# Three decay rows copied by GpSimd instead of VectorE, and one pair's query transposes moved two tiles earlier

## The chip, the cores and the metric

The kernel runs on one core of a Trainium2 chip. The core has five engines that take their instructions in order and wait for one another through semaphores: TensorE (PE, with its weight loads shown apart as PEld), VectorE (DVE), ScalarE (ACT), GpSimd (POOL) and SyncE (SP). The metric is the device time of one execution in microseconds (us). Most of it is the span that the profile shows; a little lies around the span.

## The reference

Eight batches of eight heads of causal attention with a forgetting gate (576 positions, head size 64), and behind it an MLP of 512 to 2048 to 512 on the 4608 tokens:

```python
scores = scale * np.matmul(q, k.transpose(0, 1, 3, 2))
cum = np.cumsum(np.log(np.clip(f, 0.0001, 1.0)), axis=-1)
scores = scores + cum[:, :, :, None] - cum[:, :, None, :]      # causal part only
attn = exp(scores - max) / (sum + 1e-09)
x = (attn @ v) as (B * S, H * D)
h = x @ w_in
out = (h - np.tanh(h)) @ w_out
```

## The kernel before

**The decay.** The scores are one matrix product over 67 rows: 64 rows of the head and three more that bring in the decay. K carries a high part of `cum`, a low part and ones; Q carries two rows of minus ones and the high part. `KT[0]` and `QT[0]` hold the 67 rows for each head of batch 0. At the start ACT takes the logarithm of `f` (L184), VectorE sums it up (the scan, L187) and makes the two parts `chi` (L189) and `clo` (L190), 67 partitions by 576. Head 0 is served first: partitions 64 to 66 of `clo` are its three K rows, and VectorE copies them into `KT[0]` (L191, a 3x576 copy). The rows of heads 1 to 7 are laid out by three DMAs in `bulk()`: the high and the low rows of K from SP (L211, L213), the high row of Q from GpSimd's queue (L212).

**Pairs and tiles.** The heads are worked through in pairs, 32 in all; pair p is heads 2c and 2c+1 of batch b. The loop over `p` (L658) emits a slot for each pair: seven score tiles, `scores(b, c, ti)`, and between them whatever else is due. Tiles 0 to 2 belong to the pair's first head, tile 3 is the tail of both heads (the last 64 keys, written to `EL`), tiles 4 to 6 belong to the second head. Each tile is one or two products on PE (L352), a mask product in batch 0 (L355) and an exponential on ACT (L361) that reads the PSUM bank and writes the tile `e`. Two PSUM banks are shared by the score tiles of batch 0, and a third, `tr`, by every third tile, by the tail of slot 0 and by products that nobody reads (`unread`, L566).

**Turning queries and keys.** Batch 0 comes in rows, and `trans()` turns a pair's queries or keys: six transposes on PE (L298) into a PSUM bank, then two copies of 64x576 (L309 on ACT, L311 on VectorE), for the even and the odd positions. The string `copies` says which engine takes which half ("AV": ACT first, VectorE second). Strings listed in line 314 emit only the first half at once and put the second into the list `LATER`, which `rest()` empties. In slot 0 the keys of pair 1 are turned behind tile 2, the queries of pair 2 behind tile 5; from slot 1 on, the queries of pair p+2 behind tile 5 and the keys of pair p+1 behind tile 0.

**What feeds it.** GpSimd issues the loads of q, k, v and the weights (`load_qk`, L102; `load_v_block`, L131; `load_win`, L222) from one queue, in the order in which they are emitted: heads 0 to 3 of q and k, three loads of v, a mask (L169), the high row of Q (L212), then heads 4 and 5 of q (needed by the turn of pair 2's queries), heads 4 and 5 of k, heads 6 and 7, and the blocks of v.

`start()` turns pair 0, emits its first two score tiles and fills PE with `unread` while the decay is made; `bulk()` follows, then the slots. From slot 4 on the MLP's products fill PE.

Of the kernel before, what the change touches and what calls it, by code (L numbers as in the profile page):

```python
# [21 lines left out]
def kernel(  # L22
# [10 lines left out]
    nc = tc.nc  # L33
    P = 128

    B, H, S, D = q.shape
    NH = B * H
# [3 lines left out]
    NPAIR = H // 2  # L41
# [28 lines left out]
    def m_bank(name):  # L70
        while M_AT[0] % 3 in KEPT:
            M_AT[0] += 1
        M_AT[0] += 1
        return ps_m.tile([P, 512], FP32, tag=f"m{(M_AT[0] - 1) % 3}", name=name)
# [18 lines left out]
    qn, kn = ([t[0:S // NT6, :].rearrange("p (h n d) -> p h n d", h=H, n=NT6) for t in raw] for raw in (qraw, kraw))  # L93
    qb, kb = ([t[:, 0:NJ * DM].rearrange("p (n e) -> p n e", n=NJ) for t in raw] for raw in (qraw, kraw))
    vn = [qkp.tile([P, NJ, H, VW], FP16, tag=f"vn{i}", name=f"vn{i}") for i in range(2)]
    QT = [qkp.tile([D + 3, H, S], FP16, tag=f"QT{i}", name=f"QT{i}") for i in range(2)]
    KT = [qkp.tile([D + 3, H, PITCH], FP16, tag=f"KT{i}", name=f"KT{i}") for i in range(2)]
# [3 lines left out]
    def load_qk(dst, src, b, h0, h1):  # L101
        nc.gpsimd.dma_start(  # L102
            out=dst[b % 2][:, h0:h1, :, :].rearrange("p h n d -> p h (n d)"),
            in_=src[b, h0:h1, :, :].rearrange("h (p n) d -> p h (n d)", n=NT6))
# [25 lines left out]
    def load_v_block(b, n, h0, h1):  # L130
        nc.gpsimd.dma_start(out=vn[b % 2][:, n, h0:h1, 0:D],  # L131
                            in_=v[b, h0:h1, n * P:(n + 1) * P, :].rearrange("h p d -> p h d"))
# [3 lines left out]
    NX = NH + 3  # L136
# [23 lines left out]
    chi = cst.tile([NX, S], FP16)  # L160
    clo = cst.tile([NX, S], FP16)
# [26 lines left out]
                                 op0=ALU.mult, op1=ALU.add)  # L188
    nc.vector.tensor_scalar(out=chi, in0=cum, scalar1=mul_k, scalar2=add_k, op0=ALU.mult, op1=ALU.add)  # L189
    nc.vector.scalar_tensor_tensor(out=clo, in0=cum, scalar=mul_l, in1=chi, op0=ALU.mult, op1=ALU.subtract)  # L190
    nc.vector.tensor_copy(out=KT[0][NH:NX, 0, 0:S], in_=clo[NH:NX, :])  # L191

    def aug_rows(b):
        i, h0 = b % 2, 0 if b else 1
        hs = slice(b * H + h0, (b + 1) * H)
        return [(KT[i][D:D + 1, h0:H, 0:S], chi[hs, :]), (KT[i][D + 1:D + 2, h0:H, 0:S], clo[hs, :]), (QT[i][D + 2:D + 3, h0:H, :], chi[hs, :])]

    def load_aug(b):
        for to, of in aug_rows(b):
            nc.sync.dma_start(out=to, in_=of)  # L200

    def const_rows(i):
        h0 = 1 - i
        nc.sync.dma_start(out=QT[i][D:D + 2, h0:H, :], in_=minus16[0:2 * (H - h0), :])
        nc.sync.dma_start(out=KT[i][D + 2:D + 3, h0:H, 0:S], in_=ones16[0:H - h0, :])
# [1 line left out]
    const_rows(0)  # L207

    def bulk():
        (k_hi, chi_0), (k_lo, clo_0), (q_hi, _) = aug_rows(0)  # L210
        nc.sync.dma_start(out=k_hi, in_=chi_0)  # L211
        nc.gpsimd.dma_start(out=q_hi, in_=chi_0)  # L212
        nc.sync.dma_start(out=k_lo, in_=clo_0)  # L213
        load_qk(qn, q, 0, 4, 6)
        load_qk(kn, k, 0, 4, 6)
        load_qk(qn, q, 0, 6, H)
        load_qk(kn, k, 0, 6, H)
        for n in range(NJ - 1):
            load_v_block(0, n, 2, H)
# [67 lines left out]
    def trans(b, c, src, dst, early, copies, split=False):  # L287
        pn, g3 = S // NT6, NT6 // 2
        if early:
            t32 = m_bank("t32")  # L290
        elif KEPT and src is kn:
            t32 = ps_m.tile([P, UW], FP32, tag=f"m{KEPT[0]}", name="t32")
        else:
            t32 = ps_tr.tile([P, UW], FP32, tag="tr", name="t32")
        t16 = t32.bitcast(FP16)[:, 0:2 * S // 2].rearrange("p (a g n) -> p a g n", a=2, g=g3)
        for a in range(2):
            for g in range(g3):
                nc.tensor.transpose(out=t16[:, a, g, :],  # L298
                                    in_=src[b % 2][:, 2 * c + a, 2 * g:2 * g + 2, :],
                                    identity=id16[0:pn, 0:pn])  # L300
        parts = [(a, e) for a in range(2) for e in range(2)] if split else [(slice(0, 2), e) for e in range(2)]

        def copy(a, e, eng):
            if split:
                a = slice(a, a + 1)
            to = dst[b % 2][0:D, 2 * c:2 * c + 2, e:S:2].rearrange("d a (p g) -> d a p g", g=g3)[:, a]
            of = t16[e * D:(e + 1) * D, :, :, :].rearrange("d a g p -> d a p g")[:, a]
            if eng == "A":
                nc.scalar.activation(out=to, in_=of, func=AF.Copy)  # L309
            else:  # L310
                nc.vector.tensor_copy(out=to, in_=of)  # L311

        todo = [lambda a=a, e=e, eng=eng: copy(a, e, eng) for (a, e), eng in zip(parts, copies)]
        now = 1 if copies in ("VA", "Vv") else 2
        for fn in todo[:now]:
            fn()
        if now == 1:
            LATER.extend(todo[now:])
        return todo[now:]
# [54 lines left out]
    AV = {}  # L374
# [193 lines left out]
    pairs = [(b, c) for b in range(B) for c in range(NPAIR)]  # L568
# [22 lines left out]
    def att_items(p):  # L591
        def put(fn, *args):
            items.append((lambda: fn(*args), True))

        items = []
        here = pairs[p] if p < len(pairs) else None
        before = pairs[p - 1] if 0 < p <= len(pairs) else None
        after = pairs[p + 1] if p + 1 < len(pairs) else None
        early = p < NPAIR
        for ti in range(len(TILES)):  # L600
            if here and (p > 0 or ti > 1):
                put(scores, *here, ti)
            if p == 1 and ti == 6:
                items.append((lambda: const_rows(1), False))
                items.append((lambda: load_aug(1), False))
            if p == 0 and ti in (2, 5, 6):
                put(unread, {2: 6, 5: 4, 6: 2}[ti])
            if p == 1 and ti == 3:
                put(last)
            for load in LOADS.get((p, ti), ()):  # L610
                items.append((load, False))
            at_q, at_k = (1, 2) if p == 0 else (None, 0) if early else (0, 2) if p == NPAIR else (0, 3)
            if ti == 5 and p < NPAIR - 1:
                put(trans, *pairs[p + 2], qn, QT, True, "VV")
            if p in (2 * NPAIR - 1, 2 * NPAIR, 2 * NPAIR + 1) and (ti % 2 or ti == 0):
                items.append((rest, False))
            if p in (2 * NPAIR - 1, 2 * NPAIR) and ti % 2 == 0:
                pair = pairs[2 * NPAIR + 2 * (p - 2 * NPAIR + 1) + ti // 4]
                put(trans, *pair, *((kn, KT) if ti % 4 else (qn, QT)), False, "VA")
            if ti == at_q and p < 2 * NPAIR - 1:  # L620
                put(trans, *after, qn, QT, early, "VV")
            if p == NPAIR:
                if ti in (4, 5):
                    put(mlp1, 0, ti - 4, 1)
                    items.append((rest, False))
            if ti == at_k and p < 2 * NPAIR - 1 and p != NPAIR:
                put(trans, *after, kn, KT, early, "AV" if p in (0, 2) else "VV")
            if p == NPAIR:
                if ti == 0:
                    put(turn, *pairs[1])  # L630
                elif ti == 1:
                    put(turn, *pairs[p - 2])
                    put(values, *before)
                    put(mlp1, 0, 0, 0)
                elif ti == 2:
                    put(mlp1, 0, 1, 0)
                    put(turn, *before, True)
                    put(trans, *after, kn, KT, early, "Vv")
            elif early and ti in (2, 4) and before:
                put(values, *before, (ti // 2 - 1,))  # L640
            elif not early and ti == 2 and before:
                put(values, *before, (0, 1), p == NPAIR + 2)
            if p < NPAIR:
                if ti == 1 and p == 2:
                    put(turn, *pairs[0], True)
            elif p > NPAIR and ti == 3:
                items.append((release, False))
                put(turn, *before)
        return items
# [5 lines left out]
    at = 0  # L655
    start()
    bulk()
    for p in range(len(pairs) + 1):  # L658
        b, c = divmod(p, NPAIR)
        items = att_items(p)  # L660
# [53 lines left out]
```

## Time and profile before

| what | us |
| --- | --- |
| median of 3 runs (338.79 to 338.88) | 338.80 |
| the profiled execution, its own time | 338.77 |
| its span in the profile | 337.1 |
| around the span (338.77 - 337.1) | 1.67 |
| PE idle before the first score product, for VectorE's copy into K | 0.92 |
| POOL busy between 5 and 16 us | 10.86 of 11 |

The granted clock of TensorE is 1.00 in every stretch. The table's last two rows come from the view of waits and from the busy times by stretch. A line of the chain or the timeline begins with the start and the duration in us; square brackets give the idle time of the engine before the instruction and what ended it. A mean duration in a group is in ns.

### The profile page before, as it was taken

The numbers are of one execution on the slowest core, as the hardware profiler recorded it, in microseconds if no ns is written. First come the engines' busy times: TensorE is split into PE (matmuls) and PEld (weight loads), VectorE is DVE, ScalarE is ACT, GpSimd is POOL, SyncE is SP. The second block draws the span as 40 slices with busy tenths as digits, with TensorE's granted clock in tenths as the row PEclk, the third lists the DMA queues.
The fourth block names the chain that finished last, engine by engine and source line by source line (L and its number), as shares of the span: only waits on it lengthen the run. The fifth ranks groups of instructions, "written<-read, shape, count | busy, mean of one in ns | idle before, by whom it ended". The sixth has DMA issues, their size and how long they took to land.

```text
span 337.1 us, 8726 instructions
## 1 busy us (share of the span) xinstructions
PE 330.0 (98%) x3313; PEld 235.6 (70%) x3313; DVE 260.8 (77%) x509; ACT 233.2 (69%) x438; POOL 163.2 (48%) x321
## 2 busy tenths in 40 slices
PE   8899999999999999999999999999999999999996
PEld 8775558875687558845888888656865686486485
DVE  7998986659887886778867896788668866966865
ACT  6997777978977886788677867787558733632630
POOL 8977467775667564767377637722322210000000
PEclk9999999999999999999999999999999999999999
DMA  9999999999979997999899999990130022002003
GB/s 113 143 203 202 186 198 165 184 159 172 142 87 190 136 134 72 164 152 139 94 122 187 118 112 117 163 132 18 51 113 2 19 65 97 2 31 95 0 12 116
DMA packets 147468, 38.82 MB, mean 115 GB/s; under 512 B 128181, under 2 KB 146335, under 8 KB 147426
## 3 DMA queue, kind: packets, MB, share of 16 engines
q0 software_dynamic: 94528, 18.37, 75.5%
q1 hardware_dynamic: 52892, 19.89, 32.4%
q8 instruction: 26, 0.43, 0.6%
q14 instruction: 16, 0.13, 0.2%
q10 hardware_dynamic: 6, 0.01, 0.0%
HBM read 36.85 MB, written 9.44 MB: 137 GB/s over the span
## 4 chain that ended last, share of the span: by engine, by line
PE 90%; DVE 7%; ACT 2%; issue 1%; ACTq 0%
PE hps L451 36%; PE ops L517 29%; PE ps L352 11%; PE av L389 8%; PE ops L492 4%; DVE KT L311 2%; DVE QT L311 1%; PE t L298 1%; ACT e L361 1%; DVE xn L400 1%; DVE gq L462 0%; DVE TQ L187 0%; ACT th L456 0%; PE x L417 0%; DVE clo L190 0%
## 5 line engine op out<-in xcount | busy, mean ns | idle before, releaser
L451 PE MATMUL hps<-XR,win 128*128 128x512 f16 (+1 forms) x640 | 140.7, 357 | 0.3 <-DVE gq L462 0.3
L456 ACT ACTIVATE th<-hps 128x512 f32<-128x512 f32 x144 | 86.6, 602 | 55.5 <-PE hps L451 53.5
L361 ACT ACTIVATE e<-ps 128x512 f16<-128x512 f32 x192 | 110.2, 597 | 8.9 <-PE ps L352 7.4
L462 DVE TENSOR_TENSOR gq<-hps,th 128x512 f16<-128x512 f32 x144 | 98.0, 687 | 23.6 <-ACT th L456 22.0
L371 POOL TENSOR_SCALAR_AFFINE_SELECT e<-e 128x128 f16<-128x128 f16 x168 | 60.7, 364 | 71.5 <-ACT e L361 68.7
L451 PEld LDWEIGHTS <-win 128*128 128x128 f16 x640 | 57.7, 97 | 49.0 <-issue 1.1
L352 PE MATMUL ps<-QT,KT 67*128 67x64 f16 (+4 forms) x384 | 76.5, 276 | 2.0 <-DVE KT L311 1.4
L517 PEld LDWEIGHTS <-gq 128*128 128x128 f16 x640 | 60.3, 97 | 11.1
L517 PE MATMUL ops<-wout,gq 128*128 128x256 f16 x512 | 63.2, 272 | 0.0
L352 PEld LDWEIGHTS <-KT 67*128 67x128 f16 x384 | 36.4, 98 | 23.4 <-DVE KT L311 2.0
L389 PEld LDWEIGHTS <-e 128*128 128x128 f16 x896 | 32.3, 97 | 3.6
L389 PE MATMUL av<-vn,e 128*128 128x65 f16 x896 | 33.6, 193 | 0.0
L517 PE MATMUL ops<-W,sq 128*128 128x256 f16 x256 | 31.2, 272 | 0.0
L131 POOL DMA_DIRECT2D vn<-in_v_dram x32 | 28.0, 877 | 6.5 <-DMA win<-in_moe_w_in_dram 2.9
L400 DVE TENSOR_TENSOR xn<-av,rs 128x640 f16<-128x640 f32 x32 | 26.4, 825 | 1.3 <-DVE rs L399 0.2
L517 PEld LDWEIGHTS <-sq 128*128 128x128 f16 x256 | 24.1, 97 | 3.4
L108 POOL DMA_DIRECT2D kn<-in_k_dram x25 | 21.2, 848 | 2.1 <-issue 1.8
L108 POOL DMA_DIRECT2D qn<-in_q_dram x25 | 21.2, 848 | 1.8 <-issue 1.4
L371 POOL TENSOR_SCALAR_AFFINE_SELECT el<-el 128x128 f16<-128x128 f16 x28 | 9.3, 333 | 26.1 <-ACT el L361 25.8
L398 DVE TENSOR_SCALAR rs<-av 128x10 f32<-128x10 f32 x32 | 5.2, 163 | 18.2 <-PE av L389 17.0
L532 ACT ACTIVATE m<-ops 128x512 f32<-128x512 f32 x16 | 9.5, 596 | 10.9 <-PE ops L517 10.9
L484 DVE TENSOR_TENSOR gq<-gq 128x512 f16<-128x512 f16 x32 | 17.1, 533 | 0.0
(83 smaller groups left out, 311.8 us busy)
## 6 DMA issues: line engine op xcount, KB each, us to landing
out_dram<-ost SPq DMA_DIRECT2D x34, 256.0 KB
vn<-in_v_dram POOLq DMA_DIRECT2D x24, 128.0 KB, 6.2
qn<-in_q_dram POOLq DMA_DIRECT2D x20, 128.0 KB, 5.0
kn<-in_k_dram POOLq DMA_DIRECT2D x20, 128.0 KB, 5.6
win<-in_moe_w_in_dram POOLq DMA_DIRECT2D x2, 1024.0 KB, 11.8
wout<-in_moe_w_out_dram POOLq DMA_DIRECT2D x2, 1024.0 KB, 15.6
XR<-xn SPq DMA_TRANSPOSE x56
qn<-in_q_dram POOLq DMA_DIRECT2D x6, 144.0 KB, 4.6
```

Of the source, the lines that this page charges most:

```text
L108: nc.gpsimd.dma_start(out=dst[b % 2][0:pn, n, :].rearrange("p (h d) -> p h d", h=H), in_=src[b, :, n * P:n * P + pn, :].rearrange("h p d - ...
L131: nc.gpsimd.dma_start(out=vn[b % 2][:, n, h0:h1, 0:D], in_=v[b, h0:h1, n * P:(n + 1) * P, :].rearrange("h p d -> p h d"))
L352: nc.tensor.matmul(out=ps[:, col:col + n], lhsT=kt[0:rows, h, j * P:(j + 1) * P], rhs=qt[0:rows, h, i0:i0 + n], start=True, stop=cut == 0)
L361: nc.scalar.activation(out=e[:, lo:hi], in_=ps[:, lo:hi], func=AF.Exp, bias=-SHIFT, scale=qscale)
L371: nc.gpsimd.affine_select(out=view, in_=view, compare_op=ALU.is_ge, fill=0.0, base=0, pattern=pat, channel_multiplier=-1)
L389: nc.tensor.matmul(out=av[:, a, ib, :], lhsT=E.pop((b, c, a, j, ib)), rhs=vn[b % 2][:, j, 2 * c + a, 0:D + 1], start=(j == 0), stop=(j == ib))
L400: nc.vector.tensor_tensor(out=xn.rearrange("p i (a d) -> p a i d", a=2), in0=av[:, :, :, 0:D], in1=rs.to_broadcast([P, 2, NJ, D]), op=ALU. ...
L451: nc.tensor.matmul(out=hps[:, o:o + n], lhsT=win[:, ci, ft * P:(ft + 1) * P], rhs=XR[:, ci, t:t + n], start=(ci == 0), stop=(ci == NCH - 1))
L456: nc.scalar.activation(out=th, in_=hps, func=AF.Tanh, scale=-1.0)
L462: nc.vector.tensor_tensor(out=GQ[(u, i)][:, half, kt, :], in0=hps, in1=th, op=ALU.add)
L484: nc.vector.tensor_tensor(out=LHS[name](u, i)[:, ks], in0=LHS[x](u, i)[:, ks], in1=LHS[y](u, i)[:, ks], op=op)
L517: nc.tensor.matmul(out=ps[:, m, :], lhsT=LHS[lhs](u, kt // 4)[:, kt % 4, m * P:(m + 1) * P], rhs=rhs[:, kt, :], start=(fresh and (apart or ...
```

## The change

Three edits in the prologue and slot 0. First, the copy of head 0's three K rows goes from VectorE to GpSimd, and the DMA of Q's high rows, which `bulk()` issued, is now issued by GpSimd just ahead of that copy; the loads of heads 4 to 7 follow both. Second, the turn of pair 2's queries goes from behind tile 5 to behind tile 3 of slot 0, still on two VectorE copies. Third, of pair 1's keys only ACT's half is emitted at once; VectorE's half ("v" in "Av") is put into `LATER`, and so is the second half of pair 2's queries ("Vv"). `rest()` follows, so that VectorE's order in slot 0 becomes: queries of pair 2, first half; keys of pair 1, second half; queries of pair 2, second half.

```diff
-    nc.vector.tensor_copy(out=KT[0][NH:NX, 0, 0:S], in_=clo[NH:NX, :])
+    nc.gpsimd.dma_start(out=QT[0][D + 2:D + 3, 1:H, :], in_=chi[1:H, :])
+    nc.gpsimd.tensor_copy(out=KT[0][NH:NX, 0, 0:S], in_=clo[NH:NX, :])
...
     def bulk():
-        (k_hi, chi_0), (k_lo, clo_0), (q_hi, _) = aug_rows(0)
+        (k_hi, chi_0), (k_lo, clo_0), _ = aug_rows(0)
         nc.sync.dma_start(out=k_hi, in_=chi_0)
-        nc.gpsimd.dma_start(out=q_hi, in_=chi_0)
         nc.sync.dma_start(out=k_lo, in_=clo_0)
...
-        now = 1 if copies in ("VA", "Vv") else 2
+        now = 1 if copies in ("VA", "Vv", "Av") else 2
...
-            if ti == 5 and p < NPAIR - 1:
+            if ti == 5 and 0 < p < NPAIR - 1:
                 put(trans, *pairs[p + 2], qn, QT, True, "VV")
...
-                put(trans, *after, kn, KT, early, "AV" if p in (0, 2) else "VV")
+                put(trans, *after, kn, KT, early, "Av" if p == 0 else "AV" if p == 2 else "VV")
+            if p == 0 and ti == 3:
+                put(trans, *pairs[2], qn, QT, True, "Vv")
+                items.append((rest, False))
```

## The prediction

> **What bounds it now.** I read the page first, then the chain of work that ended last (0 to 60 us), then the timeline of 5 to 31 us, then the landing of single loads.
>
> ```profile
> span 337.1 us, 8726 instructions
> PE 330.0 (98%) x3313; PEld 235.6 (70%) x3313; DVE 260.8 (77%) x509; ACT 233.2 (69%) x438; POOL 163.2 (48%) x321
> ```
>
> PE's 98% hides the stage that matters here. The chain is on VectorE, with two steps on ACT and short ones on PE, from 0.9 to 26.09 us, and on PE for most of the time after it:
>
> ```profile
> 7.76 0.30 DVE KT L191
> 8.09 0.47 DVE KT L311
> 8.58 0.49 DVE KT L311
> 9.12 0.39 PE ps L352
> ...
> 11.38 0.81 ACT KT L309
> 12.22 0.81 DVE KT L311
> 13.05 0.79 DVE QT L311
> 13.86 0.81 DVE QT L311
> ...
> 26.09 0.45 PE x L417 x5
> ```
>
> All three edits lie between 7.7 and 14.7 us, so what counts is by how much the work at 26.09 us moves; the rest is taken to move with it. The reader should see L191 on the chain, and that VectorE's half of the keys waits for ACT's half. The timeline shows who else is full:
>
> ```profile
> 7.70 0.68 POOL L102 DMA_DIRECT2D qn<-in_q_dram  x1
> ...
> 12.20 3.39 ACT L361 ACTIVATE e<-ps 128x512 f16<-128x512 f32 x6
> 12.22 0.81 DVE L311 COPY KT<-t 64x576 f16<-64x576 f16 x1 [0.34 <-ACT KT L309]
> ...
> 16.50 1.68 ACT L361 ACTIVATE e<-ps 128x512 f16<-128x512 f32 x3 [0.19 <-PE ps L352]
> ...
> 28.41 0.60 ACT L361 ACTIVATE e<-ps 128x512 f16<-128x512 f32 x1 [0.98 <-PE ps L352]
> ```
>
> ACT runs from 9.60 to about 27 us with one gap of 0.19 us. It is nearly as tight as VectorE, so a late score tile costs as much as a late copy.
>
> **Edit 1, the copy to GpSimd.** VectorE loses 8.09 - 7.76 = 0.33 us. Its second K copy then ends at 8.74 instead of 9.07, and the first score product starts at 8.79 instead of 9.12. ACT is busy with pair 0's queries until 7.30 + 2.01 = 9.31, so the exponentials start at 9.31 instead of 9.60: the gain is 0.29 us.
>
> No copy on GpSimd is in the trace. The nearest rows are its memsets and selects:
>
> ```profile
> L586 POOL MEMSET KT<- 67x512 f16 x1 | 0.6, 599 | 0.0
> L169 POOL TENSOR_SCALAR_AFFINE_SELECT late<-late 128x128 f16<-128x128 f16 x1 | 0.5, 546 | 0.0
> L587 POOL MEMSET vn<- 64x528 f16 x1 | 0.5, 533 | 0.1
> L147 POOL TENSOR_SCALAR_AFFINE_SELECT id<-id 128x128 f16<-128x128 f16 x1 | 0.3, 294 | 0.7 <-DVE id L146 0.7
> ```
>
> The memsets took 599 ns for 512 elements and 533 ns for 528. I take 0.60 us for 576, nearest in length. The lower bound is VectorE's own 0.30 us for this copy. The upper bound takes the select's mean of 336 ns for 128 elements as all slope: 4.5 x 0.336 = 1.51 us. `clo` ends at 6.91 + 0.82 = 7.73; GpSimd answered VectorE 0.08 us late at the start (1.14 to 1.22), so the copy runs from 7.80 to 8.40. That is before 8.74, so VectorE's K copies hide it as far as score tile 0 goes.
>
> [...]
>
> **What stands behind it.** GpSimd's queue: the high rows of Q keep their place (issued at 7.17, as now), but the load of heads 4 and 5 of q goes from 7.70 to about 8.42, 0.72 us later, and so do heads 4 and 5 of k, heads 6 and 7, the v blocks and the first half of `win`. Those others have cover: k heads 4 and 5 landed at 8.37 + 3.6 = 11.97 and are turned at 13.78; the last v block at 12.70 + 4.9 = 17.6, first used at 18.32 (0.72 us, and the use moves too); `win` at 16.05 + 10.1 = 26.15, used at 27.28. The load of q heads 4 and 5 loses its cover, because edit 2 wants it sooner:
>
> ```profile
> L102 POOL DMA_DIRECT2D qn<-in_q_dram x1: 675/675/675, 7.7 to 7.7; - x1
> DMA to landing us min/median/max: 3.4/3.4/3.4
> ```
>
> It landed at 7.70 + 3.4 = 11.10 and was used at 12.57. The first load of the program, with nothing ahead of it, took 3.5 us, so 3.4 looks like a floor, not a queue. I forecast 8.42 + 3.4 = 11.82, and PE starts 0.07 later (first load: 1.55 + 3.5 = 5.05, weight load at 5.12): 11.89. Bounds for the landing: 11.10, if transfers ahead of it set it; 8.42 + 4.7 = 13.1, if it takes what loads with others in flight took.
>
> **Edit 2, the transposes behind tile 3.** PE gets there at 11.42 at the latest. The second half of tile 3 waited from 11.21 to 11.33 with no engine to wait for; I read that as head 1's low rows, issued by SP at 7.76, which don't move, so the 0.29 us gained may be lost here already. In either case PE stands still until 11.89, and queued behind it are tiles 4, 5 and 6 of pair 0, on which ACT waits. Six transposes take 0.27 us (12.57 to 12.84), so tile 4 starts at 12.16 and its exponential 0.48 us later (9.12 to 9.60): 12.64 instead of 12.20.
>
> **Edit 3, the order of the copies.** VectorE fills its idle 0.34 us only if the transposes are there. From 11.89 the first copy can start at 11.89 + 0.46 = 12.35 (9.80 to 10.26 is the pattern). With 0.81 each: queries 12.35 to 13.16, keys to 13.97, queries to 14.78 (14.67 before). Pair 1's first tile needs those keys: 14.02 instead of 13.50. Its exponential follows at 14.50 instead of 13.98.
>
> **Sum.** ACT is 0.52 us late at 13.98, and has no more idle time than 0.19 us, itself spent waiting for PE, which is late with it. VectorE's own stream is only 0.1 us late at 14.7, but its division for pair 0 (16.35) waits for PE's value products, which stand behind the late score tiles in PE's queue. So about 0.5 us reaches 26.09. Against the profiled execution: 338.77 + 0.52 = 339.29; its time is 0.03 below the median of the runs, so I say 339.3. With the copy at 0.30 us the landing is 11.52, PE starts at 11.59 and the same steps give +0.22; with 1.51 us the first tile starts 0.24 late and the transposes at 12.80: +1.43.
>
> **Rivals.** (a) *The load is there in time*: its landing is set by transfers ahead of it (the v load issued last before it landed at 10.7, Q's high rows at 10.87) and stays at 11.10. For it: the DMA engines show 9 tenths busy from 7 to 8.7 us. Against it: they fall to 4 to 6 tenths from 8.75 to 9.1, so the queue had run dry. Then VectorE's order works: first copy at 11.42 + 0.46 = 11.88, keys done at 13.50, tile 0 of pair 1 no later than now; with tile 3 moving up by 0.29 us, a gain of about 0.25. That is 338.5; at best both VectorE gains are earned, 0.33 + 0.34 = 0.67, 338.1. This one isn't slower.
>
> (b) *The copy is held up*: GpSimd's select of `late` took 546 ns while VectorE's `chi` ran to 6.88, and 294 ns for the same shape at 1.22; it ended 0.15 us behind `chi`. If VectorE's K copies hold GpSimd's copy likewise to 8.74, it ends at 9.35: first tile 0.28 late, the load issued 1.67 late, transposes near 12.85, +1.5: 340.3. It decides from a copy end of 8.74 on. Against it: between 7.76 and 8.38 GpSimd issued a load in 675 ns beside VectorE's copies.
>
> [...]
>
> (c) *The delay is absorbed*: only VectorE's 0.1 us counts and ACT's lateness ends in its idle 0.98 us at 27.4. For it: the chain names VectorE up to 26.05. Against it: PE's order ties the division to the score tiles. 338.9.
>
> **How the numbers follow.** Forecast 0.52 (338.9 to 339.8), (a) 0.17, (b) and longer waits 0.19, (c) 0.12. A measurement of this kernel tells about 0.2% from no change, 0.68 us: below 338.12 is faster, above 339.48 slower. Slower: all of (b) and nearly half of the forecast's share, since the landing can only be later than its floor, 0.19 + 0.24 = 0.43. Faster: under half of (a), 0.07. Within: 0.50. The range runs from the middle of (a) to (b): 338.3 to 340.4.
>
> **What would show it.** GpSimd's copy at 7.8, about 0.6 us long; the load of q heads 4 and 5 issued near 8.4 and landing near 11.8; PE idle before the transposes of pair 2's queries from 11.4 to 11.9; ACT idle ahead of tile 4, its exponential near 12.6; pair 1's first tile near 14.0; the first score product at 8.8. It is wrong if the load lands by 11.4, if the transposes wait for something other than the load, or if the starts at 26 us don't move as those at 14 do.

## The result, and the profile after

The changed kernel takes 339.64 us as a median of 22 executions (339.35 to 343.80); the kernel before takes 338.82 (338.79 to 339.10, also 22). The ratio is 1.0040 with a 95% interval of 1.0026 to 1.0054: slower. The medians are 0.82 us apart. The ratio of the means is larger, because four of the 22 executions took 342.35 to 343.80; what these are is told further down.

The page of the profiled execution (339.81 us) shows what the chain now holds: three DMAs that were not on it, while VectorE's share falls. The last line below is the same line of the page before.

```profile
span 338.1 us, 8728 instructions
PE 330.7 (98%) x3313; PEld 236.3 (70%) x3313; DVE 260.6 (77%) x508; ACT 233.2 (69%) x438; POOL 162.8 (48%) x322
...
PE 87%; DVE 5%; DMA 4%; ACT 2%; issue 1%; POOL 0%; ACTq 0%; POOLq 0%
...
PE 90%; DVE 7%; ACT 2%; issue 1%; ACTq 0%
```

Lines from the timelines of the changed kernel that start between 7.8 and 14.3 us (start, duration, engine, line, operation, operands):

```profile
7.88 0.66 POOL L192 COPY KT<-clo 3x576 f16<-3x576 f16 x1 [0.17 <-DVE clo L190]
...
8.49 0.67 POOL L102 DMA_DIRECT2D qn<-in_q_dram  x1
...
8.76 0.38 PE L352 MATMUL ps<-QT,KT 67*128 67x512 f16 x1 [0.17 <-DVE KT L311]
...
11.31 0.19 PE L352 MATMUL ps<-QT,KT 67*128 67x64 f16 x1 [0.16 <-DMA QT<-chi]
...
12.04 0.43 PE L298 MATMUL t<-id,qn 96*128 96x96 f16 x6 [0.52 <-DMA qn<-in_q_dram]
...
12.51 0.80 DVE L311 COPY QT<-t 64x576 f16<-64x576 f16 x1 [1.01 <-PE t L298]
12.79 3.52 ACT L361 ACTIVATE e<-ps 128x512 f16<-128x512 f32 x6 [0.74 <-PE ps L355]
...
14.20 0.39 PE L352 MATMUL ps<-QT,KT 67*128 67x512 f16 x1 [0.16 <-DVE KT L311]
```

Read it from the top. GpSimd's copy is 0.66 us long and in time: the first score product starts at 8.76 instead of 9.12. The load behind it leaves at 8.49 instead of 7.70, and TensorE waits for it at the transposes that were moved up: 0.52 us of idle TensorE, 1.01 us of idle VectorE (it had 0.34 before) and 0.74 us of idle ACT. Pair 1's first tile, 13.50 before, starts at 14.20.

The chain of waits of the same execution, its first part and a later one:

```profile
7.88 0.60 POOL KT L192
8.49 3.51 DMA qn<-in_q_dram
12.04 0.44 PE t L298 x6
12.51 0.80 DVE QT L311
13.34 0.81 DVE KT L311
14.20 0.39 PE ps L352
...
26.81 0.45 PE x L417 x5
...
207.71 7.89 DMA XR<-xn
215.60 0.04 issue
215.64 0.38 PE hps L451
```

The turn at L417 that began at 26.09 before begins at 26.81: the prologue's loss, 0.72 us. It then stays the same for 188 us: set beside each other, ACT's instructions in the two traces are 0.70 to 0.74 us apart from 14 us up to 213 us. Of four MLP products that ran in one go from 213.95 before, three now start at 214.68, and the fourth waits until 215.64 for a DMA transpose of XR. The distance is 1.04 to 1.06 us from there to the end. That transpose was issued at 207.71 against 206.98 before, so its issue had moved only with the rest. It took 7.89 us, at least 0.2 us more than before, where the fourth product started at 214.60 without a wait; the traces don't show why.

### The profile page after: what moved, and what is told of

Same layout as the page of the kernel before. It is cut to its first block, busy times and chain, and to the rows that moved or that the text cites. A ratio compares the mean times of both kernels' runs of the same rounds, so it can differ in the third digit from the quotient of the medians.

```text
span 338.1 us, 8728 instructions
## 1 busy us (share of the span) xinstructions
PE 330.7 (98%) x3313; PEld 236.3 (70%) x3313; DVE 260.6 (77%) x508; ACT 233.2 (69%) x438; POOL 162.8 (48%) x322
## 4 chain that ended last, share of the span: by engine, by line
PE 87%; DVE 5%; DMA 4%; ACT 2%; issue 1%; POOL 0%; ACTq 0%; POOLq 0%
PE hps L451 36%; PE ops L517 27%; PE ps L352 11%; PE av L389 8%; PE ops L492 4%; DMA XR<-xn 2%; PE t L298 1%; ACT e L361 1%; DMA qn<-in_q_dram 1%; DVE KT L311 1%; DMA KT<-chi 1%; DVE xn L400 1%; DVE QT L311 1%; DVE gq L462 0%; DVE TQ L187 0%
## 5 line engine op out<-in xcount | busy, mean ns | idle before, releaser
L371 POOL TENSOR_SCALAR_AFFINE_SELECT e<-e 128x128 f16<-128x128 f16 x168 | 59.8, 359 | 72.5 <-ACT e L361 70.3
```

The lines of the kernel that those rows point to most:

```text
L371: nc.gpsimd.affine_select(out=view, in_=view, compare_op=ALU.is_ge, fill=0.0, base=0, pattern=pat, channel_multiplier=-1)
```

## The experiments

Theory L: the copy delays the load of q heads 4 and 5, the moved transposes need that load sooner, and this makes the prologue's whole loss. Rivals: O, the new order of VectorE's copies makes pair 1's keys late whatever the load does; S, what comes after 28 us follows from any shift of the phase; W, the load of `win`, late by as much, is what the products at 27 us run into. Each kernel ran beside the kernel before, whose medians were 338.79, 338.83 and 338.84 us in the three sets. One execution of each kernel was profiled.

**The load ahead of the copy** (e1), the undoing of the suspected delay:

```diff
     load_v_head(0, 0)
-    load_v_head(0, 1)
+    load_qk(qn, q, 0, 4, 6)
...
-        load_qk(qn, q, 0, 4, 6)
+        load_v_head(0, 1)
         load_qk(kn, k, 0, 4, 6)
```

> The change with one line moved: the load of q heads 4 and 5 takes the place in GpSimd's queue of the v load for head 1 (issued at 5.7 us), and that v load takes the place behind the copy. Theory L (the load is late because the copy stands ahead of it, and all the loss up to 14 us comes from that): the load lands well before 11.3, TensorE has no idle time before the transposes of pair 2's queries, pair 1's first score tile starts at 13.3 to 13.55 instead of 14.20, and the run is 338.5 to 338.85 us. Theory O (the new order of VectorE's copies makes pair 1's keys late whatever the load does): pair 1's first tile stays past 13.9 and the run at 339.3 or more. Theory S (what comes later, 0.3 us at 214 us and the few runs near 342.5, follows from the moved phase alone): long runs are possible here too, without the prologue's loss.

Measured: 339.32 us (338.87 to 340.40), ratio 1.0014 (1.0005 to 1.0022). Two lines of TensorE's timeline in the prologue, and one from 29 us:

```profile
11.20 0.42 PE L298 MATMUL t<-id,qn 96*128 96x96 f16 x6
...
13.40 0.39 PE L352 MATMUL ps<-QT,KT 67*128 67x512 f16 x1 [0.17 <-DVE KT L311]
...
29.05 0.39 PE L451 MATMUL hps<-XR,win 128*128 128x512 f16 x1 [1.68 <-DMA win<-in_moe_w_in_dram]
```

The transposes start at 11.20 with no wait and pair 1's first tile at 13.40, 0.10 us earlier than in the kernel before and 0.80 earlier than in the changed one. That is L's figure for the place, and O is out. The total is a miss. The profiled execution is the slowest of the eleven (340.40), and in it the products stood 1.68 us for `win`, whose landing took 11.9 us after its issue and 10.1 in the kernel before. What held the other executions isn't shown.

**Edit 1 alone** (e2): the copy on GpSimd and the DMA ahead of it; transposes and copies as before.

```diff
-    nc.vector.tensor_copy(out=KT[0][NH:NX, 0, 0:S], in_=clo[NH:NX, :])
+    nc.gpsimd.dma_start(out=QT[0][D + 2:D + 3, 1:H, :], in_=chi[1:H, :])
+    nc.gpsimd.tensor_copy(out=KT[0][NH:NX, 0, 0:S], in_=clo[NH:NX, :])
...
```

(A second hunk takes the same DMA out of `bulk()`.)

> Edit 1 alone: the three rows copied by GpSimd, the DMA of Q's high rows ahead of it; transposes and copies as before. Theory L: the load lands at 12.0 as with the whole change, but is needed only near 12.3, so nothing waits for it; the first score product starts at 8.76, the exponentials at 9.34 instead of 9.60, and the gain of 0.26 us is kept: 338.5 to 338.65. Theory O says the same. A theory that the copy itself costs (by a lock or by the loads of heads 6, 7 and v that are 0.8 us later) expects 338.9 or more.

Measured: 339.12 us (338.78 to 341.56), ratio 1.0027 (1.0009 to 1.0044): a miss. TensorE's timeline in this kernel:

```profile
11.39 0.19 PE L352 MATMUL ps<-QT,KT 67*128 67x64 f16 x1 [0.24 <-DMA QT<-chi]
...
12.32 0.42 PE L298 MATMUL t<-id,qn 96*128 96x96 f16 x6
...
13.25 0.38 PE L352 MATMUL ps<-QT,KT 67*128 67x512 f16 x1
...
27.55 0.82 PE L451 MATMUL hps<-XR,win 128*128 128x512 f16 x3 [0.35 <-DMA win<-in_moe_w_in_dram]
```

In the prologue it does what was expected: pair 1's first tile at 13.25, 0.25 us ahead. The load landed at 12.0 and was needed at 12.3, so nothing waited. In this execution (338.88, below the median) the gain is lost at 27.55, where the products come sooner and `win`, issued 0.76 us later, lands 1.36 us later (27.51 against 26.15).

**Edits 2 and 3 alone** (e3): the diff of the change without its first two hunks.

> Edits 2 and 3 alone: transposes of pair 2's queries behind tile 3 and the new order of copies; the three rows stay on VectorE and the load is issued at 7.70. Theory L: the load lands at 11.1, TensorE gets to the transposes at 11.4 and doesn't wait; pair 1's first tile is within 0.1 us of 13.50, and the run within 0.15 us of the kernel before (338.7 to 338.95). Theory O: pair 1's first tile is 0.4 us late or more and the run is at 339.2 or above.

Measured: 338.91 us (338.85 to 339.43), ratio 1.0003 (0.9994 to 1.0011): no difference, as L expects. The transposes start at 11.46 without a wait, pair 1's first tile at 13.61, 0.11 us late, and that is the end of it. So neither half of the change costs 0.7 us by itself: edit 1 makes the load late where it doesn't matter, edits 2 and 3 make it matter. With the wait that the trace of the changed kernel names, and with e1, this shows L for the prologue.

**A late start and nothing else** (e6): VectorE's copy of the rows three times.

```diff
-    nc.vector.tensor_copy(out=KT[0][NH:NX, 0, 0:S], in_=clo[NH:NX, :])
+    for _ in range(3):
+        nc.vector.tensor_copy(out=KT[0][NH:NX, 0, 0:S], in_=clo[NH:NX, :])
```

> The kernel before with the copy of the three rows done three times by VectorE (two more of 0.33 us), nothing else: the whole stream of work starts 0.66 us later, while the loads are issued as before. Theory S: 0.66 us late up to 214 us and then more, about 1.0 us at the end, and now and then a run of 342 to 344: a median near 339.6 to 339.8. If the later part of the loss is the change's own (its later loads), the run is 339.45 and no long runs come.

Measured: 339.60 us (339.50 to 343.68), ratio 1.0035 (1.0016 to 1.0054). The exponentials began 0.77 us late, and the profiled execution ended 0.91 us late. A shift of this size by itself reaches the end whole, grows by 0.14 us at the same products near 215 us, and brings executions of 340.65 and 343.68 with it. That is S in kind; the growth in the changed kernel's profile was 0.33 us, more than twice as much.

**`win` one load earlier**, under edit 1 alone (e7), the whole change (e8), the kernel before (e9) and the load-first kernel (e11):

```diff
-             (0, 4): [lambda: load_qk(qn, q, 1, 2, 4), lambda: load_qk(kn, k, 1, 2, 4)],
-             (1, 0): [lambda: load_win(0, DFF // 2)],
+             (0, 4): [lambda: load_qk(qn, q, 1, 2, 4), lambda: load_win(0, DFF // 2)],
+             (1, 0): [lambda: load_qk(kn, k, 1, 2, 4)],
```

> Edit 1 alone, with the first half of win issued one load earlier (ahead of keys 2 and 3 of batch 1, which are not turned before 29 us). Theory W (edit 1's gain of 0.25 us is lost, and its runs scatter up to 341.5, because the load of win is 0.8 us later and the first MLP products catch up with it at 27.2 us): win lands a good 0.5 us sooner, the products at 27.0 us don't wait, the gain of 0.25 us is kept to the end: 338.5 to 338.65, with few long runs. If win is not the cause: 338.9 to 339.2 and the scatter as with edit 1 alone.

> The whole change with win issued one load earlier. Theory L says that the 0.7 us at 14 us stay, since that load comes behind all that matters there. If win also causes what the changed kernel loses beyond 0.7 us and its runs of 342 to 344, the median is 339.5 or just below and no long runs come; if not (theory S), the median stays near 339.6 and long runs come in about one of six.

> The kernel before with win issued one load earlier, a control: its products never waited for win, so 338.7 to 338.9. Any gain of the two kernels above that shows here as well is not the change's.

> The change with the load of q heads 4 and 5 ahead of the copy, and win issued one load earlier. In the profile of the run without the second edit the prologue was 0.08 us ahead at 14 us and the first MLP products waited 1.68 us for win. Theory W: that wait goes or shrinks below 0.3 us, and the run is 338.65 to 338.85. Against it: 339.2 or more, if the load of win takes as long wherever it is issued.

Measured: e7 339.11 us (338.55 to 341.31), ratio 1.0013 (1.0000 to 1.0025); e8 339.76 (339.39 to 343.15), 1.0034 (1.0017 to 1.0051); e9 338.88 (338.77 to 340.38), 1.0004 (0.9996 to 1.0013); e11 339.20 (338.90 to 339.77), 1.0012 (1.0004 to 1.0021). In none of these four profiles did a product wait for `win`. The earlier issue is only part of that: in e11 it came 0.60 us earlier than in e1, and the landing 2.58 us earlier (26.43 against 29.01). The medians didn't follow: e7 and e11 are misses, and W does not account for what edit 1 and the load-first kernel lose. e8 keeps its 0.73 us at 14 us and a long execution, so `win` has no part in the changed kernel's loss. (In e8's profile Q's high rows are late as well: TensorE waits 0.58 us for them up to 11.72, and the load of q lands at 12.02.) In e7's profiled execution (339.73) other transfers took the gain. Its timeline of TensorE, and below it its chain at 73 us:

```profile
12.65 0.43 PE L298 MATMUL t<-id,qn 96*128 96x96 f16 x6 [0.17 <-DMA qn<-in_q_dram]
```

```profile
65.78 7.46 DMA XR<-xn
73.24 0.04 issue
73.28 0.38 PE hps L451
```

The same load of q landed 4.1 us after its issue here, 3.5 in e2, so even the transposes in their old place had to wait; and at 73.28 a product waited for XR, as one did at 215 us in the changed kernel and does at 215.56 here too. A third wait, 0.22 us at 105.51, is for VectorE.

**Edit 1, load first, `win` earlier** (e12), the candidate for a better kernel, and **one MLP step fewer in slot 6**, under the change (e13) and under e12 (e15):

```diff
-    TAKE = (0, 0, 0, 0, 2, 7, 6, 6, 6, 8, 8, 7, 7)
+    TAKE = (0, 0, 0, 0, 2, 7, 5, 6, 6, 8, 8, 7, 7)
```

> A version to beat both: edit 1 alone (transposes and copies as before), the load of q heads 4 and 5 ahead of the copy, win one load earlier. Theories L and W together: neither the transposes nor the first MLP products wait for a load, the 0.25 us gained at 9.4 us stay up to 28 us and beyond: 338.5 to 338.65. If the transposed tiles of the later stages cut in (theory S), 338.8 to 339.2 as a median, with the profile showing products that wait for XR near 73 or 215 us.

> The whole change, with one MLP step less given to slot 6 (5 instead of 6), so that all later MLP steps come one step, about 1.1 us, later in the order and the last one at the end. Theory S (the loss beyond 0.72 us and the long runs are MLP products that catch up with the DMA transposes of XR): the 0.3 us at 215 us go and the long runs too; the median is near 339.5, the runs within 339.4 to 339.8. Against it: long runs in one of six as before.

> The first kernel of this call with one MLP step less in slot 6. Theory S: no products wait for XR, so the 0.25 us of the prologue reach the end: 338.5 to 338.65 with a narrow spread. If the moved order of MLP steps costs by itself, more than the first kernel of this call.

Measured: e12 339.25 us (338.54 to 341.18), ratio 1.0017 (1.0004 to 1.0030); e13 344.86 (343.01 to 349.18), 1.0174; e15 343.95 (343.89 to 345.90), 1.0152. e12 had the lowest single execution of all, 338.54, and no better median than the others: a miss. Its profiled execution (338.88) never had the gain that was to be kept:

```profile
7.35 2.06 PE L566 MATMUL idle<-warm 128*128 128x128 f16 x34
...
9.25 0.38 PE L352 MATMUL ps<-QT,KT 67*128 67x512 f16 x1
```

The first score product starts at 9.25, against 8.76 in the changed kernel, because TensorE is busy with `unread` products until then. Of the 47 that stand ahead of the first transposes, the last 32 take 3.62 us here, 3.13 in the changed kernel and 2.59 in the kernel before, where TensorE then stands idle for 0.92 us ahead of the first score product. So the kernel before has cover for a slow start of TensorE, and edit 1 uses up 0.36 us of it (9.12 to 8.76). How often a start is this slow isn't shown.

e13 and e15 are failures as tests of S: the moved steps leave TensorE standing for 2.5 us, up to 53 us, behind an exponential, which cost far more than the wait they were to remove. They show something else, below.

**A second copy on GpSimd** (e14), the suspected cost doubled:

```diff
     nc.gpsimd.tensor_copy(out=KT[0][NH:NX, 0, 0:S], in_=clo[NH:NX, :])
+    spare = cst.tile([NX, S], FP16)
+    nc.gpsimd.tensor_copy(out=spare[NH:NX, :], in_=clo[NH:NX, :])
```

> The whole change with a second copy of the same 3x576 rows on GpSimd, into a tile that nobody reads, right behind the first: the load of q heads 4 and 5 is issued 0.62 us later still (9.1 us), the first score product isn't touched. Theory L: the load lands near 12.6, the transposes start there, pair 1's first tile at 14.8 instead of 14.20, and the run is 0.6 us longer than the changed kernel: 340.2 to 340.4. Theory O, or a cost of the copy by itself: pair 1's first tile stays near 14.2.

Measured: 339.86 us (339.67 to 343.94), ratio 1.0050 (1.0028 to 1.0072). The load left at 9.11, 0.62 later, but landed in 3.0 us instead of 3.5, so the transposes started at 12.16 and pair 1's first tile at 14.32: 0.12 later, not 0.6. The median is a miss too (340.2 to 340.4 expected). As a dose it is too small to decide between L and its rivals, and it shows that a landing need not move by as much as its issue. The execution that was profiled is one of the long ones, though (343.94 us). Its busy times by stretch of 1 us (length, then busy time and count of PE, PEld, DVE, ACT and POOL, then the granted clock, the DMA share and GB/s):

```profile
11.00:12.00 1.00, 0.31 (x6) 0.14 (x3) 0.50 (x1) 1.00 (x3) 1.00 (x3) 1.00 1.21 176
12.00:13.00 1.00, 0.84 (x12) 0.63 (x13) 0.38 (x1) 0.13 (x2) 1.00 (x2) 1.00 1.07 158
13.00:14.00 1.00, 0.82 (x13) 0.65 (x10) 0.97 (x2) 0.99 (x2) 1.00 (x2) 1.00 1.18 158
14.00:15.00 1.00, 0.84 (x8) 0.41 (x6) 0.95 (x2) 0.60 (x1) 1.00 (x3) 0.69 1.64 158
15.00:16.00 1.00, 1.00 (x11) 0.75 (x9) 0.47 (x1) 0.60 (x1) 1.00 (x2) 0.50 2.33 151
```

While TensorE waits for the load it is busy for 0.31 us of the first stretch; 2.4 us after that stretch its granted clock falls to 0.50. The trace's record of the clock has it there from 14.38 for 10.24 us. With that, the long executions can be read: each execution's mean granted clock is recorded. In the changed kernel the four above 342 us have 0.985 to 0.990, the other 18 have 0.998 or more; with the low clock taken as e14's 0.50, a mean of 0.990 over 340.7 us is an estimated 0.010 x 2 x 340.7 = 6.8 us of it, and 0.985 is 10.2 us. The kernel before never fell below 0.998 in the executions that stand beside the experiments. e6, e8 and e14 have executions at 0.995 or less too (two, one and three of twelve); e1, e3, e7, e9, e11 and e12 have none. But e2 has two of twelve at 0.995 (341.07 and 341.56), though TensorE didn't wait for the load of q in its profile. So a wait at the moved transposes (0.85 us, up to 12.16) comes 2.2 us ahead of the halved clock in e14; that it is the cause isn't shown. What lowered the clock in e2, and in the changed kernel's own four, isn't shown either, as none of these was profiled. Nor is every long execution of this kind: 340.40 (e1), 341.52 (e2), 341.31 (e7) and 341.18 (e12) ran at a mean of 1.000.

## Why the prediction was right, and where it was short

The direction, the place and the steps held: the change is slower because the load, moved back by GpSimd's copy, lost its cover when the transposes moved up. The median, 339.64, is inside the range 338.3 to 340.4 and 0.34 above the forecast of 339.3. The chances were less sure than the account: 0.50 for no clear change, 0.43 for slower. Step by step:

- **The copy.** Forecast 7.80 to 8.40, measured 7.88 to 8.54 (0.66 us against 0.60), hidden behind VectorE's K copies as said; the load left at 8.49 against 8.42.
- **The landing.** Forecast 11.82, measured 8.49 + 3.51 = 12.00. The step "3.4 looks like a floor" was wrong: the same load took 3.0 us in e14 and 4.1 in e7. It is a spread, not a floor. The 0.07 us from landing to TensorE was 0.04; at the first load, from which it was read, TensorE came straight from `unread` products and had not waited.
- **The stall.** Transposes forecast at 11.89, measured 12.04; tile 4's exponential 12.64 against 12.79; VectorE's first copy 12.35 against 12.51; pair 1's first tile 14.02 against 14.20. Each is late by what the load was. The sum at 26 us was sized at 0.52 and measured 0.72: the mechanism right, the term of the load 0.2 us short.
- **The wait inside tile 3.** It is there (11.31), and it does eat most of the 0.29 us, but the trace of the changed kernel names Q's high rows, GpSimd's DMA, and not the low rows from SP that I had read into it.
- **"The rest is taken to move with it."** This is the step that failed. The profiled execution loses 0.33 us more at 215 us, where a product now waits for a DMA transpose that it didn't wait for before. And four of 22 executions, at a mean clock of 0.985 to 0.990, take some 3 us more. The forecast had no term for either. The profiled execution is 0.52 us above the forecast's 339.29, and the first is 0.33 of that; the second is why the ratio (1.0040) is larger than that of the medians (1.0024).
- **Covers.** `win` was said to have 1.1 us of cover. That held in the changed kernel, which is late itself, but not where the products came sooner (e1, e2). A cover was counted in the schedule before, and a landing that varies from 9.6 to 11.9 us between kernels doesn't keep it.

Rival (a), the load there in time, fell: the issue moved by 0.79 us and the landing by 0.93 (11.07 to 12.00). Its idea that more than the issue sets a landing has something to it, as e14's 0.11 us for 0.62 shows. The kernel nearest to its price is e1, with the load in time: pair 1's first tile 0.10 us earlier, where (a) counted on a gain of about 0.25. Rival (b), the copy held up, fell: 0.66 us (7.88 to 8.54) right beside VectorE's four copies from PSUM (L311, 7.65 to 9.62). Rival (c), the delay absorbed, fell: 0.72 us reached 213 us nearly unchanged.

What stays open: why e1, e7, e11 and e12 have medians 0.3 to 0.5 us above the kernel before and spread over 0.9 to 2.8 us, where the kernel before stays within 0.7. In the one execution of each that was profiled, the loss was a wait for `win` (e1), for q, XR and VectorE (e7), 0.18 us for VectorE at 105 us (e11) and the slow start (e12). That the landings of loads and the start of TensorE vary from one execution to the next would explain it; it was argued, not shown. No version beat the kernel before.

## What to carry to other kernels

An instruction put on a queue that also issues loads delays the loads behind it: here a copy of 0.66 us, after a wait of 0.17, moved the issue of the next load by 0.79 us and that of `win` by 0.76. Look for the load whose use is moved up by the same change, since two edits that cost the prologue little or nothing one by one (e2, e3) can meet there. A gain of a few tenths in a prologue is kept only if every just-in-time transfer later on has more cover than the gain plus the spread of its landing (e2: products 0.25 us early, `win` issued 0.76 us later and 0.60 slower to land, against a cover of 1.1). And look at the clock behind a stall on TensorE: in e14 a wait of 0.85 us was followed by 10.24 us at half clock, in an execution of 343.94 us against a median of 339.86; in e1 a wait of 1.68 us was not. A median hides this, the mean and the granted clock of each execution show it.

## What the runs showed that was not expected

In e14 the clock was halved although TensorE was busy for most of the time just ahead: the 2 us from 12 to 14, before the fall at 14.38, hold 0.84 + 0.82 = 1.66 us of busy TensorE, 83%. In e15 the fall comes at 52.29. Its stretches around it, and as the last line one of e6, in which the clock was kept, read (columns as above):

```profile
48.00:50.00 2.00, 2.00 (x12) 0.95 (x11) 1.92 (x5) 1.38 (x4) 1.43 (x4) 1.00 1.33 202
50.00:52.00 2.00, 0.33 (x4) 0.14 (x2) 1.97 (x4) 0.31 (x1) 0.91 (x2) 1.00 1.44 199
52.00:54.00 2.00, 1.18 (x5) 0.69 (x5) 0.88 (x2) 1.76 (x4) 0.69 (x2) 0.57 1.46 199
54.00:56.00 2.00, 2.00 (x15) 1.41 (x13) 0.37 (x1) 0.10 (x1) 0.29 (x1) 0.50 1.58 179
56.00:58.00 2.00, 2.00 (x12) 1.37 (x10) 0.43 (x1) 1.41 (x2) 1.13 (x2) 0.50 2.47 148
58.00:60.00 2.00, 2.00 (x27) 1.74 (x26) 0.79 (x1) 0.60 (x1) 0.94 (x2) 0.72 2.55 142
60.00:62.00 2.00, 2.00 (x38) 1.76 (x35) 1.18 (x3) 0.59 (x2) 1.18 (x3) 1.00 2.14 126
...
9.00:10.00 1.00, 0.18 (x3) 0.11 (x2) 0.95 (x3) 0.31 (x1) 1.00 (x2) 1.00 1.11 128
```

In e15 the fall lies within the wait of 2.5 us that ends near 53; in e14 it comes 2.2 us after the wait has ended. The clock stays low for 6.83 us in e15 and for 10.24 us in e14, though TensorE is busy without a break from 54 us on in the one and from 15 us on in the other.

Nor is it the busy share of a single stretch that decides. In e6 TensorE is busy for 0.18 of the 1 us from 9 to 10, less than the 0.31 us from 11 to 12 in e14, and the clock is 1.00 in every stretch read, up to 20 us. In e1 TensorE waits 1.68 us for `win`, up to 29.05, and the mean clock of that execution is 1.000. What else counts, and why only some executions are hit, isn't shown.
